# Eighteen rows of one head and batch to a partition, and key sums in four row tiles

## The chip, the cores and the metric

The kernel runs on one core of a Trainium2 chip. The metric is device time in microseconds of one execution, without the profiler; the number given for a kernel is the median of its runs. A profile is one execution of its own, taken with the hardware profiler on; its span runs from the first instruction to the last.

## What is computed

A linear attention ("hedgehog" features) feeds a spectral mixing layer. There are 8 batches, 8 heads, 576 rows of a sequence and head dimension 64; the second stage sees 8 x 576 rows of 512 channels.

```python
def phi(x):                                   # 64 -> 128 -> 256 features
    proj = np.einsum('bhsd,df->bhsf', x, w_phi)
    proj = proj - np.max(np.abs(proj), axis=-1, keepdims=True)
    return np.concatenate([np.exp(proj), np.exp(-proj)], axis=-1)
q_p, k_p = (phi(q), phi(k))
kv = np.einsum('bhsf,bhsd->bhfd', k_p, v)     # the key sums
z = np.sum(k_p, axis=2)
num = np.einsum('bhsf,bhfd->bhsd', q_p, kv)
den = np.einsum('bhsf,bhf->bhs', q_p, z)[..., None] + 1e-06
x = (num / den)                               # then (batch, row, 512)
...
X = np.fft.rfft(x, axis=1)                    # 64 lowest modes, w_r and w_i per mode
Yr = Xr @ w_r - Xi @ w_i;  Yi = Xr @ w_i + Xi @ w_r
u = x + np.fft.irfft(Y, n=S, axis=1)
out = u + np.maximum(u @ w_ch, 0.0)
```

The weights `w_r` and `w_i` are 64 x 512 x 512 each in float32, 134 MB together; q, k and v are 9.4 MB each, and so is the output.

## The kernel before

**Units.** The attention is cut into 16 units: a unit is two heads (group `g` of 4) of two batches (pair `bp` of 4). A tile of q, k or v has 128 partitions of 18 rows of 64. Before, partition `64 h + p` holds rows `9 p` to `9 p + 8` of head `h`, first of one batch and then of the other, so a load has two runs of 9 rows (2304 B in memory) for each partition (`load`, lines 94 to 98). q and k are cast to bf16 on the way, v stays float32. The source's axes come in the order row group (128), batch (2), run (576); the tile's in the order partition (128), batch (2), run (576).

**The loop.** One loop (lines 534 to 612) runs over steps `n`, and in a step four units are at different stages. Unit `n + 2` ("R") is transposed on PE (`turn_k`, `turn_q`, copied out by ACT). Unit `n + 1` ("K") has its projections and their maxima (`rows_k`, `rows_q`: PE, then DVE) and the exponentials of the keys (`exp_k`, tiles `AB` and `ABr`, on ACT). Unit `n` ("Q") has v weighted by the maxima (`weigh_v2`, DVE, tile `va`), the queries' projections and exponentials (`cols_q`, `exp_q`, tiles `AQ` and `AQr`), the key sums (`kv`, copied out by `keep_kv` into `kvz`), and the numerators and denominators (`num`, in three parts). Unit `n - 1` ("P") goes through the forward transform (`freq`, `keep_x`). Each engine keeps the order in which the program issues its work (class `InOrder`).

**Loads and queues.** POOL issues k and q of unit `n + 4`, v of unit `n + 2` and the weights, each in the step as it stands in the loop; they share POOL's software DMA queue. v of units 0 and 1 (line 383 and 386) and of unit 15 (`load_v_parts`, line 113, in pieces of 57, 64 and 7 partitions) are issued on SP, whose queue also carries the stores. A weight tile `wt` is 1024 KB in bf16, read from 2 MB in float32; there are 64 of them, nine buffers, and some places that are free early (`home`). A tile is asked for again when a tile has been used (`some`, `next_w`).

**PSUM.** In the loop, tiles named `two` take two banks and there are two of them; tiles named `one` take one bank and there are four. A step uses `two` in this order: `rows_k(0)`, `cols_q(1)`, `rows_k(1)`, `rows_q(0)`, `rows_q(1)`, `cols_q(0)`; a use waits for the reader of the use two places before it. The key sums go to two `one` tiles, one for each head:

```python
for h in range(2):
    r = slice(64 * h, 64 * h + 64)
    pe.matmul(
        pk[h][:, i, ab, :], lhsT=self.AB[n // 8][r, ab, n % 8, :],
        rhs=self.va[r, ab, n, :],
        start=(i == ab == c == 0), stop=(i == ab == 1 and c == 8),
    )
```

so that two matmuls of 64 rows, on the two halves of PE's rows, follow each other; 72 of them for a unit.

**The second stage.** After the loop the rest of the weights is mixed in (`mix`), and between the mixes the channel products (`Channels`) and the inverse transform (`Absorb`) are done. What needs the last weights follows in `finish`, and the output rows are written in `Pair.store` on SP: pairs of row places are written as one DMA of 512 KB (in two halves for the first three pairs), and the ninth place of each partition (`n8`) in DMAs of its own. Which row of the sequence stands at which place also enters the tables of the transforms (`si`, `nine`, `tok`) and the places that `back`, `freq` and `store` name.

Of the kernel before, what the change touches and what calls it, by code (L numbers as in the profile page):

```python
# [43 lines left out]
def kernel(  # L44
# [49 lines left out]
    def load(t, src, g, bp, eng):  # L94
        eng.dma_start(
            t.rearrange("p b c d -> p b (c d)"),
            src[2 * bp:2 * bp + 2, 2 * g:2 * g + 2].rearrange("b h (p c) d -> (h p) b (c d)", c=9),
        )


    class Unit:
# [3 lines left out]
        def load_k(self):  # L105
            self.kb = pin.tile([128, 2, 9, D_], BF16, name="kb")
            load(self.kb, k, self.g, self.bp, pool)

        def load_q(self):
            self.qb = pin.tile([128, 2, 9, D_], BF16, name="qb")  # L110
            load(self.qb, q, self.g, self.bp, pool)

        def load_v_parts(self):
            self.vn = pin.tile([128, 2, 9, D_], F32, name="vn")
            dst = self.vn.rearrange("p b c d -> p b (c d)")
            src = v[2 * self.bp:2 * self.bp + 2, 2 * self.g:2 * self.g + 2].rearrange(
                "b h (p c) d -> (h p) b (c d)", c=9)
            for p0, p1 in ((0, 57), (57, 121), (121, 128)):
                sp.dma_start(dst[p0:p1], src[p0:p1])

        def load_v(self, eng=pool):
            self.vn = pin.tile([128, 2, 9, D_], F32, name="vn")
            load(self.vn, v, self.g, self.bp, eng)

        def turn(self, src, dst, flat, part):

            rows = src.rearrange("p i c d -> p (i c d)")
            lo, hi = ((0, 4), (4, 9))[part]
            ptr = one([128, hi - lo, 128], BF16)
            for j in range(lo, hi):  # L130
                if flat or j < 4:
                    pe.transpose(ptr[:, j - lo, :], rows[:, j * 128:(j + 1) * 128], ident_b)
                elif j < 8:
                    n = 9 + 2 * (j - 4)
                    pe.transpose(ptr[:, j - lo, :], rows[:, n * 64:n * 64 + 128], ident_b)
                else:
                    for i in range(2):
                        pe.transpose(ptr[64 * i:64 * i + 64, j - lo, :], src[:, i, 8, :], ident_b)
# [51 lines left out]
        def weigh_v2(self):  # L190
# [3 lines left out]
            for ab in range(2):  # L194
                dve.tensor_tensor(
                    out=self.va[:, ab, :, 0:64], in0=self.vn.rearrange("p i c d -> p (i c) d"),
# [4 lines left out]
        def kv(self):  # L201
            pk = [one([128, 2, 2, 65]) for h in range(2)]
            for i in range(2):
                for ab in range(2):
                    for c in range(9):
                        n = 9 * i + c
                        for h in range(2):
                            r = slice(64 * h, 64 * h + 64)
                            pe.matmul(
                                pk[h][:, i, ab, :], lhsT=self.AB[n // 8][r, ab, n % 8, :],  # L210
                                rhs=self.va[r, ab, n, :],
                                start=(i == ab == c == 0), stop=(i == ab == 1 and c == 8),
                            )
            self.pk2 = pk

        def keep_kv(self):
            for h in range(2):
                act.copy(self.kvz[:, h], self.pk2[h])
# [41 lines left out]
        def exp_q(self, i):  # L260
            if i == 0:
                self.AQ = []
            if i < 2:
                t = pm.tile([128, 2, 2, 2, 2, 64, 2], BF16, name="AQ", bufs=3)
            else:
                t = pm.tile([128, 2, 2, 128], BF16, name="AQr", bufs=1)
            for ab in range(2):
                if i < 2:
                    o = t[:, ab].rearrange("f c j h p a -> f a c (j h) p")
                    src = self.pa.rearrange("f c (a j) (h p) -> f a c (j h) p", a=2, h=2)  # L270
                else:
                    o, src = t[:, ab], self.pa
                act.activation(o, src, ACT.Exp, scale=1.0 - 2.0 * ab)
            self.AQ.append(t)

        def num(self, n0):

            pn = one([128, 6, 65])
            for n in range(n0, n0 + 6):
                h = n % 2  # L280
                if n < 16:
                    i, c = n // 8, n % 8 // 2
                    for ab in range(2):
                        pe.matmul(
                            pn[:, n - n0, :],
                            lhsT=self.AQ[i][:, ab, c % 2, c // 2, h].rearrange("f p a -> f (p a)"),
                            rhs=self.kvz[:, h, i, ab, :], start=(ab == 0), stop=(ab == 1),
                        )
                else:
                    for i in range(2):  # L290
                        r = slice(64 * i, 64 * i + 64)
                        for ab in range(2):
                            pe.matmul(
                                pn[r, n - n0, :],
                                lhsT=self.AQ[2][:, ab, i, 64 * h:64 * h + 64],
# [9 lines left out]
        def freq(self):  # L305
            g, bp = self.g, self.bp
            px = one([128, 4, 2, 2, 32])
            for i in range(2):
                for out, d, t in ((px[:, 0:4:3, :, i], 0, slice(0, 2)),
                                  (px[:, 2, :, i], 1, 0), (px[:, 1, :, i], -1, 1)):  # L310
                    for c in range(5):
                        n = 8 * i + 2 * c if c < 4 else 16
# [79 lines left out]
    for p0 in (0, 64):  # L392
        pool.iota(si[p0:p0 + 64, 4:5], [[1, 1]], base=8, channel_multiplier=9)
# [3 lines left out]
    pool.iota(nine.bitcast(I32), [[9, 64]], base=0, channel_multiplier=0)  # L397
# [22 lines left out]
    dve.tensor_scalar_mul(out=odd[:, 1:2], in0=odd[:, 0:1], scalar1=-0.5)  # L420
# [113 lines left out]
    for n in range(-2, len(units) + 1):  # L534
# [55 lines left out]
        elif R and n + 4 == len(units):  # L590
            kept = pin.tile([128, 2, 9, D_], BF16, name="kb").rearrange(
                "p b c d -> p (b c d)")[:, 0:1024].rearrange("p (f m) -> p f m", m=8)
# [84 lines left out]
    def inverse_tables():  # L677
# [11 lines left out]
        for i in range(2):  # L689
            dve.tensor_scalar_add(out=tok[:, 512 + 64 * i:576 + 64 * i], in0=nine, scalar1=8.0)  # L690
# [75 lines left out]

    def back(p, c, bp, table, src, r, start):

        if c < 8:
            pe.matmul(p, lhsT=table[r, c % 4, :], rhs=src[r, 2 * bp + c // 4, :],  # L770
# [98 lines left out]
    class Pair:  # L869
# [32 lines left out]
        def sums(self, side, a):  # L902
            (bp, n), at, z = self.items[a], self.at(side, a), self.z(side)
            start = not self.based(side)
            if self.straight:
                pe.matmul(at, lhsT=CM[n // 4][:, n % 4], rhs=ends[z], start=start,
# [29 lines left out]
        def store(self):  # L936
# [3 lines left out]
            for p in parts:  # L940
                a = slice(p[0], p[-1] + 1)
                self.add(a)
                if self.n8:
                    sp.dma_start(
                        bass.AP(tensor=out.tensor, offset=out.offset + (2 * bp * S_ + 8) * DMODEL,
# [206 lines left out]
```

## Time and profile before

| | |
|---|---|
| time, median of 3 runs | 431.36 us (430.62 to 431.5) |
| the profiled execution | 430.94 us, span 428.7 us |
| PE, DVE, ACT, POOL busy | 321.2, 303.6, 300.6, 127.8 us |
| bytes moved by DMA | 97.71 MB in 50040 packets, 228 GB/s on the mean |
| read from HBM, written | 163.64 MB, 9.44 MB |
| mean granted TensorE clock | 0.942 |
| key sums' matmuls (64 x 128, 65 columns) | 1152, mean 199 ns each, overlapping |
| ACT: `AQ`, `AB`, 128x1024 | 1347 ns (x64), 1051 ns (x64) |
| ACT: `kvz` copies, 128x260 | 438 ns (x32) |
| ACT: `AQr`, 128x256 | 384 ns (x32) |
| k, q, v loads on POOL's queue, issue to landing, median | 21.4, 19.7, 25.1 us |
| v on SP's queue, units 0 and 1, issue to landing | 4.6 us |

A busy time is the sum of an engine's instructions where they don't overlap; DMA issues, waits and register work are not in it. The 40 slices show each engine's busy share in tenths. The chain of waits is followed back from the last instruction: at each step to what released it. "Issue to landing" has the time in the queue in it, not only the transfer. A DMA leaves one record for each packet of data, and beside them small records of 4 B, with which it reports that its part on one DMA engine is done. bytes are counted where they are written: a weight's 4096 B of float32 become a packet of 2048 B.

### The profile page before, as it was taken

The page shows a single profiled execution, that of the slowest core. Times are in us where ns is not written, and L with a number is a line of the kernel's source. Part 1 is how long each engine was busy: PE and PEld are TensorE (multiplying, and loading weights), DVE is VectorE, ACT ScalarE, POOL GpSimd, SP SyncE. Part 2 cuts the span into 40 slices and gives each one's busy share as a digit, 9 for nine tenths or more (in the row PEclk, how much of TensorE's full clock was granted, in tenths as well). Part 3 has the DMA queues.
Part 4 walks back from the last instruction along what each step waited for, and adds up shares of the span by engine and source line. Part 5 has one row for each costly group of instructions (what it writes and reads, how often), then busy time and mean ns, then how long its engine had stood idle before and what let it go on. Part 6 is the DMA issues. An engine that isn't in the chain of part 4 may idle for free.

```text
span 428.7 us, 10215 instructions
## 1 busy us (share of the span) xinstructions
PE 321.2 (75%) x4243; PEld 195.5 (46%) x4291; DVE 303.6 (71%) x592; ACT 300.6 (70%) x490; POOL 127.8 (30%) x167
## 2 busy tenths in 40 slices
PE   1666676678696677786795767867899789878994
PEld 1345555456364445554564545543454333333321
DVE  6668668766776776877877858868645546964695
ACT  3788788896887996977978848766644335553883
POOL 6232132123121213213122321220122037691661
PEclk9989799989999998998989969898999989999998
DMA  9999999999999999999999999999999999999798
GB/s 215 209 211 211 237 214 238 219 231 238 240 210 230 220 238 238 238 210 240 210 240 218 232 240 233 212 211 213 212 212 212 212 212 212 212 212 194 190 398 344
DMA packets 50040, 97.71 MB, mean 228 GB/s; under 512 B 2379, under 2 KB 11723, under 8 KB 49995
## 3 DMA queue, kind: packets, MB, share of 16 engines
q0 software_dynamic: 45152, 85.27, 101.6%
q1 hardware_dynamic: 4682, 11.73, 7.6%
q8 instruction: 33, 0.54, 0.5%
q10 hardware_dynamic: 160, 0.07, 0.1%
q14 instruction: 13, 0.10, 0.1%
HBM read 163.64 MB, written 9.44 MB: 404 GB/s over the span
## 4 chain that ended last, share of the span: by engine, by line
DMA 34%; PE 24%; ACT 22%; DVE 14%; issue 4%; POOL 1%; ACTq 0%; POOLq 0%; DVEq 0%
DMA wt<-in_moe_w_i_dram 28%; ACT AQ L37 9%; PE one L37 8%; PE pt L37 8%; DMA kb<-in_k_dram 6%; ACT AB L37 6%; DVE m L37 6%; PE two L37 5%; PE pp L37 3%; ACT qT L37 2%; ACT XT L37 2%; DVE xw L37 2%; DVE mk L37 1%; DVE mT L37 1%; DVE xs L37 1%
## 5 line engine op out<-in xcount | busy, mean ns | idle before, releaser
L37 ACT ACTIVATE AQ<-two 128x1024 bf16<-128x1024 f32 x64 | 80.5, 1347 | 2.2 <-PE two L37 2.1
L37 ACT ACTIVATE AB<-two 128x1024 bf16<-128x1024 f32 x64 | 62.7, 1051 | 4.5 <-DVE mk L37 4.2
L37 DVE TENSOR_REDUCE m<-two 128x8 f32<-128x1024 f32 x32 | 39.1, 1223 | 19.9 <-PE two L37 19.6
L37 POOL DMA_DIRECT2D wt<-in_moe_w_i_dram x30 | 22.2, 739 | 85.3 <-PE one L37 44.1
L37 DVE TENSOR_REDUCE mk<-two 128x8 f32<-128x1024 f32 x32 | 38.9, 1219 | 9.4 <-PE two L37 9.4
L37 ACT CAST xw<-pt 128x512 bf16<-128x512 f32 x39 | 22.9, 586 | 31.8 <-PE pt L37 31.6
L37 DVE TENSOR_TENSOR va<-vn,ee 128x1152 bf16<-128x1152 f32 x32 | 42.8, 1383 | 1.8 <-DMA vn<-in_v_dram 1.8
L37 PE MATMUL pt<-wchb,xT 128*128 128x512 bf16 x135 | 37.8, 394 | 7.2 <-DVE xT L37 2.4
L37 PE MATMUL two<-w2blk,qT 128*128 128x256 bf16 x128 | 21.9, 299 | 24.0 <-ACT AQ L37 12.3
L37 POOL DMA_DIRECT2D wt<-in_moe_w_r_dram x32 | 23.6, 739 | 52.6 <-PE one L37 25.9
L37 PEld LDWEIGHTS <-xs 128*128 128x128 bf16 x624 | 31.2, 102 | 13.3 <-issue 6.8
L37 ACT COPY qT<-one 128x512 bf16<-128x512 bf16 (+1 forms) x32 | 19.0, 642 | 20.8 <-PE one L37 20.7
L37 PEld LDWEIGHTS <-qT 128*128 128x128 bf16 x144 | 14.5, 103 | 38.2 <-issue 34.9
L37 PEld LDWEIGHTS <-XT 128*32 128x32 bf16 x584 | 16.8, 148 | 29.8 <-issue 16.9
L37 POOL DMA_DIRECT2D kb<-in_k_dram x16 | 11.4, 713 | 62.1 <-PE one L37 47.8
L37 PE MATMUL two<-mT,minus 96*128 96x512 bf16 x64 | 26.2, 410 | 2.9 <-issue 0.7
L37 DVE TENSOR_TENSOR xs<-one,rd 128x384 bf16<-128x384 f32 x48 | 26.8, 557 | 1.6
L37 PE MATMUL one<-wt,XT 128*32 128x512 bf16 x272 | 23.9, 439 | 3.4 <-ACT XT L37 3.4
L37 DVE TENSOR_TENSOR xs<-pa,xs 128x512 bf16<-128x512 f32 x27 | 17.7, 685 | 12.1 <-PE pa L37 10.3
L37 PE MATMUL one<-kvz,AQ 128*128 128x65 bf16 x512 | 25.3, 200 | 1.1 <-ACT qT L37 0.8
L37 PEld LDWEIGHTS <-AQ 128*128 128x128 bf16 x512 | 22.6, 103 | 7.0 <-issue 3.0
L37 POOL TENSOR_TENSOR xw<-rl,xw 128x512 bf16<-128x512 f32 x20 | 22.7, 1169 | 7.9 <-ACT rl L37 7.6
(161 smaller groups left out, 733.5 us busy)
## 6 DMA issues: line engine op xcount, KB each, us to landing
wt<-in_moe_w_r_dram POOLq DMA_DIRECT2D x29, 1024.0 KB, 27.7
wt<-in_moe_w_i_dram POOLq DMA_DIRECT2D x27, 1024.0 KB, 28.0
out_dram<-of SPq DMA_DIRECT2D x15, 512.0 KB, 3.6
vn<-in_v_dram POOLq DMA_DIRECT2D x13, 576.0 KB, 25.1
kb<-in_k_dram POOLq DMA_DIRECT2D x16, 288.0 KB, 21.4
qb<-in_q_dram POOLq DMA_DIRECT2D x16, 288.0 KB, 19.7
xs<-in_moe_w_i_dram POOLq DMA_DIRECT2D x2, 1024.0 KB, 23.9
out_dram<-of SPq DMA_DIRECT2D x6, 256.0 KB, 4.1
```

The lines of the kernel that those rows point to most:

```text
L37: ins = f(*args, **kwargs)
```

## The change

A partition of q, k and v now holds 18 rows of one head and one batch: partition `64 b + 32 h + p` holds rows `18 p` to `18 p + 17` of head `h` and batch `b`. The run in memory is 4608 B. The source pattern of a load is now batch (2), row group (64), run (1152), and the tile's is partition (128), run (1152). v of unit 15 is loaded in four pieces (57, 7, 57 and 7 partitions) instead of three.

A head and batch is now 32 partitions, so the key sums contract 32 rows at a time, in four row tiles: 144 matmuls for a unit. Two of the four results stand in the two banks of one `two` tile and two in `one` tiles; `keep_kv` copies them in three instructions instead of two. A step's order of `two` tiles becomes `rows_k(0)`, `cols_q(1)`, `rows_k(1)`, the sums, `rows_q(0)`, `rows_q(1)`, `cols_q(0)`.

`turn` transposes nine blocks of 128 columns for q too (ten pieces before). `exp_q` writes `AQ` with a stride of four elements (two before) and `AQr` with a stride of two (none before). The places of rows in the tables and in the output change with the layout; the stores keep their sizes, but for the ninth place, where two batch pairs are now two DMAs of 256 KB instead of one of 512 KB. Setting up the tables takes a few more small instructions on DVE. The number of rows in PE's program goes from 8562 to 10834.

```diff
     def load(t, src, g, bp, eng):
         eng.dma_start(
-            t.rearrange("p b c d -> p b (c d)"),
-            src[2 * bp:2 * bp + 2, 2 * g:2 * g + 2].rearrange("b h (p c) d -> (h p) b (c d)", c=9),
+            t.rearrange("p c d -> p (c d)"),
+            src[2 * bp:2 * bp + 2, 2 * g:2 * g + 2].rearrange("b h (p c) d -> b (h p) (c d)", c=18),
         )
...
         def load_v_parts(self):
...
-                "b h (p c) d -> (h p) b (c d)", c=9)
-            for p0, p1 in ((0, 57), (57, 121), (121, 128)):
-                sp.dma_start(dst[p0:p1], src[p0:p1])
+                "b h (p c) d -> b (h p) (c d)", c=18)
+            for p0, p1 in ((0, 57), (57, 64), (64, 121), (121, 128)):
+                sp.dma_start(dst[p0:p1], src[p0 // 64, p0 % 64:(p1 - 1) % 64 + 1])
...
             for j in range(lo, hi):
-                if flat or j < 4:
-                    pe.transpose(ptr[:, j - lo, :], rows[:, j * 128:(j + 1) * 128], ident_b)
-                elif j < 8:
-                    n = 9 + 2 * (j - 4)
-                    pe.transpose(ptr[:, j - lo, :], rows[:, n * 64:n * 64 + 128], ident_b)
-                else:
-                    for i in range(2):
-                        pe.transpose(ptr[64 * i:64 * i + 64, j - lo, :], src[:, i, 8, :], ident_b)
+                m = j if flat or j > 7 else 2 * (j % 4) + j // 4
+                pe.transpose(ptr[:, j - lo, :], rows[:, m * 128:(m + 1) * 128], ident_b)
...
         def kv(self):
-            pk = [one([128, 2, 2, 65]) for h in range(2)]
-            for i in range(2):
+            low = two([128, 2, DMODEL])[:, :, 0:130].rearrange("p h (a d) -> p h a d", a=2)
+            high = [one([128, 2, 65]) for h in range(2)]
+            out = [low[:, 0], low[:, 1]] + high
+            for i in range(3):
                 for ab in range(2):
-                    for c in range(9):
-                        n = 9 * i + c
-                        for h in range(2):
-                            r = slice(64 * h, 64 * h + 64)
+                    for n in range(8 * i, min(8 * i + 8, 18)):
+                        for p in range(4):
+                            r = slice(32 * p, 32 * p + 32)
                             pe.matmul(
-                                pk[h][:, i, ab, :], lhsT=self.AB[n // 8][r, ab, n % 8, :],
+                                out[p][:, ab, :], lhsT=self.AB[i][r, ab, n % 8, :],
                                 rhs=self.va[r, ab, n, :],
-                                start=(i == ab == c == 0), stop=(i == ab == 1 and c == 8),
+                                start=(n == ab == 0), stop=(n == 17 and ab == 1),
                             )
-            self.pk2 = pk
+            self.pk2 = low, high
 
         def keep_kv(self):
+            low, high = self.pk2
+            act.copy(self.kvz[:, :, 0], low)
             for h in range(2):
-                act.copy(self.kvz[:, h], self.pk2[h])
+                act.copy(self.kvz[:, h, 1], high[h])
...
             if i < 2:
-                t = pm.tile([128, 2, 2, 2, 2, 64, 2], BF16, name="AQ", bufs=3)
+                t = pm.tile([128, 2, 2, 2, 2, 32, 4], BF16, name="AQ", bufs=3)
             else:
-                t = pm.tile([128, 2, 2, 128], BF16, name="AQr", bufs=1)
+                t = pm.tile([128, 2, 2, 2, 32, 2], BF16, name="AQr", bufs=1)
             for ab in range(2):
                 if i < 2:
-                    o = t[:, ab].rearrange("f c j h p a -> f a c (j h) p")
-                    src = self.pa.rearrange("f c (a j) (h p) -> f a c (j h) p", a=2, h=2)
+                    o = t[:, ab].rearrange("f c b h p a -> f c a (b h p)")
                 else:
-                    o, src = t[:, ab], self.pa
-                act.activation(o, src, ACT.Exp, scale=1.0 - 2.0 * ab)
+                    o = t[:, ab].rearrange("f b h p e -> f e (b h p)")
+                act.activation(o, self.pa, ACT.Exp, scale=1.0 - 2.0 * ab)
...
                 if self.n8:
+                    for i, (bp, n) in enumerate(self.items):
+                        sp.dma_start(
...
                     sp.dma_start(
-                        bass.AP(tensor=rows.tensor,
-                                offset=rows.offset + (n % 4 + p[0]) * DMODEL,
-                                ap=[[9 * DMODEL, 64], [4 * DMODEL, 2], [1, len(p) * DMODEL]]),
+                        bass.AP(tensor=rows.tensor, offset=rows.offset + (j + p[0]) * DMODEL,
+                                ap=[[18 * DMODEL, 32], [4 * DMODEL, 4], [1, len(p) * DMODEL]]),
                         self.o[:, a].rearrange("p a e -> p (a e)"))
```

## The prediction

> **What bounds the kernel now.** I read the page first: its slices, its queues and its chain.
>
> ```profile
> span 428.7 us, 10215 instructions
> ...
> PE   1666676678696677786795767867899789878994
> ...
> DMA  9999999999999999999999999999999999999798
> ...
> q0 software_dynamic: 45152, 85.27, 101.6%
> q1 hardware_dynamic: 4682, 11.73, 7.6%
> ```
>
> No compute engine is at 9 for long; the DMA engines are, in 37 slices of 40. q0 is the queue that POOL feeds: weights, k, q and most of v. To tell a saturated queue from a busy one I read the chain in order of time:
>
> ```profile
> 200.70 25.02 DMA wt<-in_moe_w_i_dram
> 226.25 26.74 DMA kb<-in_k_dram
> 253.52 30.95 DMA wt<-in_moe_w_i_dram
> ...
> 328.49 37.24 DMA wt<-in_moe_w_i_dram
> 366.01 27.12 DMA wt<-in_moe_w_i_dram
> ```
>
> A weight tile waits 25 to 37 us between issue and landing. In the trace's completion records a 1024 KB weight tile lands 4.95 us behind the one ahead of it, so five to seven tiles stand in the queue at any time. Until 200 us the chain runs through compute instead, but behind a full queue that only shortens the queue. The last weights land at 393.2 us and 34 us of output work follow. So the time is a DMA stream of 390 us plus that tail, if compute can keep up. Whether it can, the windows say:
>
> ```profile
> core 0: us, PE busy (x) PEld busy (x) DVE busy (x) ACT busy (x) POOL busy (x), PEclk, DMA share, GB/s
> ...
> 200.00:285.00 85.00, 63.99 (x1119) 44.09 (x1121) 64.00 (x116) 63.25 (x102) 19.15 (x25) 0.91 1.13 225
> 285.00:328.00 43.00, 36.54 (x292) 18.52 (x299) 29.27 (x100) 25.32 (x45) 6.97 (x9) 0.96 1.12 212
> 328.00:366.00 38.00, 32.82 (x231) 14.85 (x233) 21.17 (x43) 16.68 (x32) 13.60 (x15) 0.96 1.12 212
> 366.00:395.00 29.00, 23.05 (x210) 10.56 (x212) 20.05 (x35) 14.95 (x29) 18.59 (x20) 1.00 1.09 209
> ```
>
> From 285 to 395 us PE works 92.4 of 110 us: compute has at most 18 us of air there. In the attention loop one step takes 15.1 us by compute (AQ starts at 71.22 and 86.34 in the chain); from the first step at 24.2 us, 16.4 steps would end at 272 us, and the stream holds the loop until 285. That is another 13 us of air.
>
> **The loads: how many engines carry them.** This part decides. Before, the source pattern of a load starts with 128 rows; after, `b (h p) (c d)` starts with the 2 batches. What does a short leading count do? The trace has two rows for it, the hardware queue's packets in the first 6.5 us and from 247 to 260 us:
>
> ```profile
> q1 hardware_dynamic: 544, 1.18, 53.7%
> ```
>
> ```profile
> q1 hardware_dynamic: 282, 0.59, 13.5%
> ```
>
> The first is v of units 0 and 1: 512 data packets and 32 four-byte completions, 16 for each DMA. The second is v of unit 15 in pieces of 57, 64 and 7 rows: 256 data packets and 26 completions, which is 3 + 16 + 7. A piece runs on as many engines as the largest number up to 16 that divides its leading count. From 252.4 us on, the 57-row piece trickles at 5 to 6 packets per half microsecond, where all pieces together had made 36: three engines, each taking one such packet (106 ns) and one weight packet (154 ns) in turn. By this reading a load that leads with 2 runs on two engines. The Trainium skill's page "DMA: Bandwidth & Descriptors", in "Why a DMA increments its semaphore by 16 and not by 1", gives this rule (the largest count up to 16 that divides the slowest dimension of both patterns), puts hardware-queue DMAs on the lowest-numbered engines and moves software ones round by a cursor; the trace agrees on 3, 16 and 7, and no row shows a leading 2.
>
> Packet prices per engine: a weight packet (2048 B written) is 4.95/32 = 154.7 ns. A k load lands 1.43 us behind the DMA ahead, 16 packets of 1152 B, 89.4 ns each. A v load takes 1.41 us, 8 packets of 4608 B, 176 ns. A merged k packet of 2304 B is not in the trace: on the line through the first two it costs 173 ns, with two of the old ones as upper bound, 179. I take 173. If all sixteen engines carried it, the merge would save (179 - 173) x 8 x 32 loads = 1.4 us. On two engines a load is 64 packets, 11.1 us, on each of them.
>
> A weight tile needs all 16 engines, so the stream ends with its most loaded engine. I assume that v of units 0 and 1 fall on the same pair (if not: 11.3 us less on it), and that the 45 software loads go round the eight pairs, 5 or 6 each. Then for that pair:
>
> - v of units 0 and 1: 2 x 64 x 176 ns = 22.5 us, where 4.0 us (1.8 to 5.8 us) stood before: +18.5.
> - v of unit 15: 40 packets x 176 ns = 7.0 for 48 x 106 ns = 5.1: +1.9.
> - 32 k and q and 13 v loads: 32 x 1.43 + 13 x 1.41 = 64.1 us become 6 x 11.1 = 66.6, or 5 x 11.1 = 55.5: +2.5, or -8.6. I take 6, since the first load is likely to start at the first pair and 45 is five rounds and five pairs.
> - PE's program grows from 8562 to 10834 rows; at 0.54 MB for the former that is 9 more 16 KB fetches, 0.95 us each, over 16 engines: +0.5.
>
> The stream: +23.4 us, bounds +1 (different pairs and 5 loads) and +23.4.
>
> **Compute, behind that stream.** k of unit 0 shares its pair with v. Packets taken in turn, its 64 need 64 x (173 + 176) = 22.3 us: it lands near 27 us instead of 7.7, and the first transpose moves from 8.75 by about 18 us (with a pair of its own, 7). Then the key sums. They now also fill a "two" tile, of which there are two:
>
> ```profile
> 75.95 2.54 ACT L37 ACTIVATE AQ<-two 128x1024 bf16<-128x1024 f32 x2
> ...
> 75.98 0.97 PE L37 MATMUL one<-va,AB 64*128 64x65 bf16 x50
> ...
> 78.54 0.60 PE L37 MATMUL two<-w2blk,qT 128*128 128x256 bf16 x4 [1.23 <-ACT AQ L37]
> ```
>
> Before, the sums start beside AQ; after, their tile is the one that AQ reads, so they start at 78.5, in the 1.23 us that PE waits. That is free, but the next tile is late: the first q projection then needs the tile of AB, free at 80.3, not AQ's, 78.5: +1.8 us. DVE's maxima, shift, and the num matmuls queue behind it: about +1.9 us a step. The sums have 72 pairs of load and matmul now, two row tiles at a time, one pair of tiles each 32 ns (1.14 us); 144 in fours take the same 1.14 us if four run beside each other, 2.28 if only two do. No row shows four row tiles; the nearest, 128*32 weight matmuls in four column tiles, start 2 ns apart, so I take 1.14. ACT: three copies for two, with 128x130 between the rows of 36 (249 ns) and 260 elements (438): about 328, +0.22 us a unit; AQr to a stride, by AQ over AB (1347/1051): 384 to 492 ns, +0.22; AQ's stride doubles, between 1051 and 1643 ns, I keep 1347. One transpose less saves PE about 60 ns. Two more store issues on SP lie under 3.6 us of landing: 0 here, 0.5 each if SP were the bound.
>
> Loop end by compute: 272 + 18 + 16 x 1.9 = 320, 35 later than 285. The second stage can win back 7 us (the waits of PE and its loads for weights there) to 18: +17 to +28 at 395. The stream's +23.4 and this meet, so the later of the two is some 25 us. 430.9 (the profiled run, 0.4 under the median of 431.36) + 25 = **456 us**. Its own range is 440 to 474: below, five loads on the pair and a pair of its own for k; above, key sums that run only two tiles at a time (1.14 x 16 = 18 us) that the second stage takes in part.
>
> **Rivals.**
> - *All loads still use sixteen engines*, because the 128 partitions of the destination decide. For it: every software DMA here shows 16 completions (1888 for 118), though none leads with less than 16. The merge then saves 1.4 us, by packet durations (107 ns for 1152 B, 173 for 2048) as much as 5.7; the code fetch costs 0.5, and the loop's 30 us of waits fit into 13 + 18 us of air. **430.0 us**, 425 at best: not slower. It decides if a load of k still lands 1.4 us behind the DMA ahead of it. 0.11.
> - *Only the hardware queue narrows*, so that k and q stay short: +18.5 + 1.9 + 0.5 - 1.4: **450 us**. For it: the 3 and the 7 are both hardware rows. 0.09.
> - *The software loads don't go round* and all fall on one pair: 45 x 11.1 = 500 us for 64.1, **890 us**. Against it: nothing in the trace piles up. 0.04.
> - *Sixteen engines, but the loop's wait breaks through*: 30 us less only the loop's 13: **447 us**. 0.02.
>
> The forecast keeps 0.74. **Range 436 to 476**: it leaves out the first and third rival and 0.05 of the forecast. 0.2%, 0.9 us, is about what a measurement tells from no change: the first rival splits into 0.07 faster and 0.04 the same; slower 0.89.
>
> **What would show it.** Two completions for v of units 0 and 1 on the hardware queue, not 16; their packets until 25 to 50 us; the first transpose after 15 us; k loads that land up to 11 us behind their neighbours, with single engines busy while others idle (a DMA row below 9); the last weight near 415. The key sums starting at AQ's end shows the tile's wait, groups of four within some 10 ns the tiles. It is wrong if k lands in 1.4 us steps, and if the row of the DMA stays at 9 with the last weight at 392.

## The result, and the profile after

The changed kernel takes 580.31 us (median of 6 runs, 578.38 to 581.33) where the kernel before takes 431.35 (6 runs, 430.62 to 431.78): a ratio of 1.3453, interval 1.3426 to 1.348. The forecast was 456 us, in a range of 436 to 476. The direction was right, the size was not: 149 us more where 25 were forecast.

The profiled execution spans 578.8 us, 150.1 more than before's 428.7. First the slices and queues of its page, beside the rows that the prediction began with:

```profile
span 578.8 us, 12582 instructions
...
PE   0025464655766648476673756657567899799995
...
PEclk9997575756768596675776668676698899899998
DMA  8629999698679998877989899999989999696498
...
DMA packets 85886, 98.02 MB, mean 169 GB/s; under 512 B 42696, under 2 KB 43848, under 8 KB 85832
...
q0 software_dynamic: 81376, 85.43, 83.6%
```

The stream is no longer the bound. q0's packets took 101.6% of the span before and take 83.6% now, the DMA row has 6s, 7s and 8s, and a weight tile lands sooner after its issue, not later. Before, then after (the last number is the median from issue to landing, in us):

```profile
wt<-in_moe_w_i_dram POOLq DMA_DIRECT2D x27, 1024.0 KB, 28.0
...
wt<-in_moe_w_i_dram POOLq DMA_DIRECT2D x27, 1024.0 KB, 16.7
```

POOL shows it too: before, its instructions wait 37 us in all for weights to land, after not at all.

So the queue empties, and something else holds the loop. The window from 200 to 285 us (PE, PEld, DVE, ACT, POOL busy, then PE's granted clock, DMA share and GB/s) shows no engine full, and PE's clock at 0.72 where it had been 0.91:

```profile
200.00:285.00 85.00, 55.06 (x970) 36.86 (x970) 44.61 (x79) 65.86 (x82) 15.97 (x20) 0.72 0.90 157
```

That is a chain in which engines take turns. The chain of waits (start, duration, what) shows it over one step of the loop, from one unit's first `AQ` to the next one's. Before:

```profile
71.22 2.39 ACT AQ L37 x2
...
76.12 2.38 ACT AQ L37 x2
...
78.54 0.61 PE two L37 x4
...
79.17 1.23 DVE m L37
...
86.34 2.39 ACT AQ L37 x2
```

And after (the key sums are many small pieces; the first is kept here):

```profile
330.07 4.65 ACT AQ L37 x2
...
337.20 4.61 ACT AQ L37 x2
...
341.85 0.20 PE two L37 x2
...
342.94 1.95 ACT AB L37 x2
...
344.93 1.03 PE two L37 x4
...
345.97 1.22 DVE m L37
...
353.14 2.40 ACT AQ L37
```

The operation that has grown most, over the whole span, before and after (count, busy time, mean ns, idle time before):

```profile
L37 ACT ACTIVATE AQ<-two 128x1024 bf16<-128x1024 f32 x64 | 80.5, 1347 | 2.2 <-PE two L37 2.1
...
L37 ACT ACTIVATE AQ<-two 128x1024 bf16<-128x1024 f32 x64 | 152.3, 2529 | 2.2 <-PE two L37 2.2
```

Three stretches are to be compared. From the first pair of `AQ` to the end of the second: 76.12 + 2.38 - 71.22 = 7.28 us before, 337.20 + 4.61 - 330.07 = 11.74 after, 4.46 more. From there to DVE's maxima of `rows_q(0)`: 0.67 before, 4.16 after, 3.49 more: the key sums and `exp_k(1)` have come into the chain, and the projection itself takes 1.03 us where it took 0.61. From there to the next `AQ`: 7.17 both times. The step has grown by 7.95 us.

The rest is at the start. In the waits of the first 60 us, PE stands still for k and q of unit 0 (total, times, longest):

```profile
PE one L37 <- DMA kb<-in_k_dram: 32.7, 1, 32.7
...
PE one L37 <- DMA qb<-in_q_dram: 7.7, 1, 7.7
```

k of unit 0 lands at 32.6 us (8.1 before) and q at 41.4 (9.5 before). v of units 0 and 1 each report two completions now, at 26.0 and 26.5 and at 40.4 and 40.9 us, where 16 each stood before: the narrow loads that the prediction had named. In slices of 1 us, from 0 to 40 us, the DMA row falls to one tenth, some two of sixteen engines, from 28 to 35 us, while q of unit 0 and v of unit 1 were still on their way:

```profile
DMA  0036659999999999997555555553111111143222
```

The three stretches can be measured for all steps and all kernels from the starts and durations in the trace. The table gives the median time; the start of the first unit's first `AQ`; the three stretches as means over the 15 steps to the last unit's first `AQ` (a: to the end of the second pair of `AQ`; b: on to the start of DVE's maxima of `rows_q(0)`; c: on to the next unit's `AQ`); the mean step; and what follows from the last of these to the span's end.

| kernel | time, us | first AQ | a | b | c | step | behind |
|---|---|---|---|---|---|---|---|
| before | 431.35 | 24.1 | 7.46 | 0.99 | 8.13 | 16.58 | 155.9 |
| after | 580.31 | 55.5 | 11.82 | 4.61 | 8.09 | 24.52 | 155.5 |
| e1: after, loads on 16 engines | 549.98 | 26.2 | 11.81 | 4.46 | 8.15 | 24.42 | 156.4 |
| e2: after, AQ without stride | 504.71 | 54.5 | 6.56 | 4.91 | 8.06 | 19.53 | 156.1 |
| e3: e1 and e2 | 468.25 | 26.3 | 6.56 | 4.58 | 7.89 | 19.02 | 156.2 |
| e4: before, key sums in `two` | 474.10 | 24.1 | 7.42 | 4.20 | 8.05 | 19.66 | 152.6 |
| e5: before, AQ at a stride of four | 504.64 | 24.0 | 11.84 | 0.92 | 8.77 | 21.53 | 154.8 |
| e7: before, strided read | 432.09 | 24.1 | 6.69 | 1.24 | 8.84 | 16.77 | 155.5 |
| e8: e1 with strided read | 470.43 | 27.0 | 6.57 | 4.55 | 7.93 | 19.04 | 155.5 |
| e9: e4, one stock of tiles | 450.62 | 24.1 | 7.41 | 3.27 | 7.57 | 18.25 | 150.5 |
| e10: e8, one stock of tiles | 466.79 | 26.1 | 6.58 | 4.07 | 8.14 | 18.79 | 154.3 |
| e11: e8, sums in pairs, early | 507.49 | 26.0 | 9.42 | 3.33 | 8.76 | 21.51 | 158.1 |
| e12: e10, sums in pairs, later | 453.39 | 25.9 | 7.18 | 1.76 | 9.15 | 18.09 | 155.3 |
| e13: e7, one stock of tiles | 432.48 | 23.0 | 6.65 | 1.23 | 8.81 | 16.69 | 157.1 |
| e14: before, loads split | 436.65 | 25.3 | 7.79 | 0.91 | 8.46 | 17.17 | 151.2 |

For the changed kernel: 31.4 us more at the start, 15 x 4.36 = 65 in stretch a, 15 x 3.62 = 54 in stretch b, nothing in c and nothing behind the loop. That is the 150 us between the spans.

### The profile page after: what moved, and what is told of

Read it like the earlier page. It is cut to its first block, busy times and chain, and to the rows that moved or that the text cites. A ratio compares the mean times of both kernels' runs of the same rounds, so it can differ in the third digit from the quotient of the medians.

```text
span 578.8 us, 12582 instructions
## 1 busy us (share of the span) xinstructions
PE 370.5 (64%) x5427; PEld 220.7 (38%) x5427; DVE 302.0 (52%) x598; ACT 375.7 (65%) x506; POOL 133.2 (23%) x167
## 3 DMA queue, kind: packets, MB, share of 16 engines
q0 software_dynamic: 81376, 85.43, 83.6%
## 5 line engine op out<-in xcount | busy, mean ns | idle before, releaser
L37 ACT ACTIVATE AQ<-two 128x1024 bf16<-128x1024 f32 x64 | 152.3, 2529 | 2.2 <-PE two L37 2.2
L37 PE MATMUL two<-va,AB 32*128 32x65 bf16 x1024 | 30.3, 236 | 56.3 <-ACT AQ L37 56.3
L37 PE MATMUL two<-qT,w2blk 128*128 128x512 bf16 x64 | 31.1, 485 | 44.9 <-ACT AQ L37 44.9
L37 PEld LDWEIGHTS <-AB 32*128 32x128 bf16 x2048 | 29.3, 124 | 62.3 <-issue 62.3
L37 POOL DMA_DIRECT2D kb<-in_k_dram x16 | 13.4, 835 | 131.4 <-PE one L37 130.5
L37 PE MATMUL two<-w2blk,qT 128*128 128x256 bf16 x128 | 32.0, 399 | 16.5 <-ACT AB L37 15.3
L37 PE MATMUL one<-ident_b,kb 128*128 128x128 bf16 x144 | 19.2, 286 | 33.0 <-DMA kb<-in_k_dram 32.7
L37 ACT COPY kT<-one 128x512 bf16<-128x512 bf16 (+1 forms) x32 | 20.0, 635 | 30.8 <-PE one L37 30.7
L37 PEld LDWEIGHTS <-xs 128*128 128x128 bf16 x624 | 31.4, 103 | 12.4 <-issue 6.8
L37 ACT ACTIVATE AQr<-one 128x256 bf16<-128x256 f32 x32 | 12.3, 457 | 34.3 <-PE one L37 34.3
L37 DVE TENSOR_TENSOR XT<-one,side 128x256 bf16<-128x256 f32 x32 | 12.1, 420 | 39.9 <-ACT XT L37 37.8
L37 PEld LDWEIGHTS <-minus 96*128 96x128 bf16 x96 | 11.8, 123 | 53.2 <-issue 50.0
```

The source lines that it names most:

```text
L37: ins = f(*args, **kwargs)
```

## The experiments

Each group ran beside the kernel before on the same chip: 431.67 us for the first to fourth, 431.81 for the fifth to eighth, 432.33 for the ninth to eleventh, 432.19 for the twelfth and thirteenth, 431.41 for the last.

### e1: the loads on sixteen engines

```diff
-        eng.dma_start(t.rearrange("p c d -> p (c d)"),
-            src[2 * bp:2 * bp + 2, 2 * g:2 * g + 2].rearrange("b h (p c) d -> b (h p) (c d)", c=18))
+        for b in range(2):
+            eng.dma_start(t[64 * b:64 * b + 64].rearrange("p c d -> p (c d)"),
+                src[2 * bp + b, 2 * g:2 * g + 2].rearrange("h (p c) d -> (h p) (c d)", c=18))
```

> After, but each load of k, q and v is two DMAs of 64 partitions, one for each batch, so that no source pattern leads with 2. If the loads' two engines are the main cause (the forecast's step): about 440, and the DMA row at 9 again. If the stride of AQ is (2529 ns for 1347): only the late start goes, k of unit 0 lands near 9 us for 32.7 and the loop keeps its step of 23.5 us: 550 to 560.

549.98 us, ratio 1.2745 (1.2699 to 1.2792): 30 us of the 149. Nearly all of it is the start (first `AQ` at 26.2 us instead of 55.5); the step hardly moves (24.42 for 24.52), which is the second case. While the loop is slow, narrow loads hide in it.

### e2 and e3: AQ written without a gap

```diff
-                    o = t[:, ab].rearrange("f c b h p a -> f c a (b h p)")
+                    o = t[:, ab].rearrange("f c b h p a -> f (c b h p a)")
+                    src = self.pa.rearrange("f c n s -> f (c n s)")
```

and the same for `AQr`; e3 has e1's loads too, and its numerators stand in the same other order as those of e2.

> After, but AQ and AQr are written without a stride, in the order in which they are read (so the numerators use rows and columns in a wrong order). If the stride is the main cause: AQ at 1050 ns, 4 x 1.5 us less in a step, 16 steps: 580 - 95 = 485, or what the two-engine loads then allow, not under 455. If it is not: 570 or more, since ACT was busy 65% only.

> After with both edits: 16 engines for the loads and AQ without a stride. What is left is the key sums' wait for their two-bank tile, 144 matmuls and a third copy. If these are hidden, as forecast for a stream of 16 engines: 425 to 432. If the wait breaks through: 435 to 450.

e2 takes 504.71 us, 1.1675 (1.1604 to 1.1745): 76 us for the order in which the elements of `AQ` and `AQr` stand, 20 us short of its first case (485). `AQ` takes 1051 ns there, so this takes off 64 x 1.48 = 95 us of ACT's work, the 0.30 us of before's own stride among it. e3 takes 468.25, 1.0851 (1.0779 to 1.0922), outside both of its cases; the two parts add up (30 + 76 of the 112). Between e2 and e3 the loads' share is 36 us, 28.2 at the start and 15 x 0.51 in the loop: in a faster loop the narrow loads are no longer quite hidden. Some 37 us remain that neither part explains.

### e4: the key sums in a two-bank tile, alone

```diff
-            pk = [one([128, 2, 2, 65]) for h in range(2)]
+            both = two([128, 2, DMODEL])[:, :, 0:260].rearrange("p h (i a d) -> p h i a d", i=2, a=2)
+            pk = [both[:, h] for h in range(2)]
```

> Before, with the key sums (two row tiles of 64, as before) in the two banks of a two tile: the wait alone. The sums then start when AQ ends, not beside it, and a step is up to 1.9 us longer. If the air of 13 and 18 us takes it: 430 to 433. If not: up to 447.

474.10 us, 1.0987 (1.0962 to 1.1013), above both cases: 42 us for a tile's place in PSUM, in the kernel before with its 72 matmuls of 64 rows. The timeline (start, duration, what; in brackets what an engine had idled for) shows how:

```profile
129.99 2.52 ACT L37 ACTIVATE AQ<-two 128x1024 bf16<-128x1024 f32 x2
132.57 1.51 PE L37 MATMUL two<-va,AB 64*128 64x65 bf16 x50 [2.47 <-ACT AQ L37]
133.73 1.94 ACT L37 ACTIVATE AB<-two 128x1024 bf16<-128x1024 f32 x2 [1.21 <-PE two L37]
...
135.72 1.01 PE L37 MATMUL two<-w2blk,qT 128*128 128x256 bf16 x4 [1.03 <-ACT AB L37]
136.77 1.23 DVE L37 TENSOR_REDUCE m<-two 128x8 f32<-128x1024 f32 x1 [4.68 <-PE two L37]
```

PE waits 2.47 us for `AQ`'s tile. Then ACT, which had nothing to do with the sums, waits 1.21 us for PE: `AB` has three buffers and a unit takes two, so `exp_k(1)` of unit `n + 1` writes the buffer that holds the first `AB` tile of unit `n`, and these sums still read it. Only when its exponentials are done may `rows_q(0)` have its tile, and it runs at 1.01 us for 0.60: PE's granted clock is 0.50 from 132.7 to 139.5 us, from the end of PE's wait of 2.47 us on (0.83 over the span, 0.94 before; the first 50 sums take 1.51 us here, 0.97 before). That the wait brings the low clock is likely, since it comes so in nearly every step, but no run shows it by itself. The table has it all in stretch b: 4.20 us for 0.99.

### e5 and e6: the price of the stride

e5 writes `AQ` in the kernel before at a stride of four elements; e6 writes the four `AQ` operations of a unit at one, two, four and eight:

```diff
+                    n = 2 ** (2 * i + ab)
+                    o = t[ab].rearrange("f c j h p a -> f (c j h p a)").rearrange("f (s n) -> f n s", n=n)
```

> The kernel before, its AQ numerators written at a stride of four elements (8 B) instead of two, nothing else changed; the numerators then stand in another order than the later matmuls read them, so the output is not the reference's. My theory: the write alone sets the price, so AQ takes 2.5 us as in the changed kernel (1.35 before), and since PE's two-bank tiles come free only at the end of AQ and AB, the loop's step grows by the whole 4 x 1.18 = 4.7 us, from 15.1 to about 19.8. 16 steps are 75 us, less the 13 us of air that the loop has and up to 18 us behind it: 475 to 493 us. Rival: ACT has room (63.25 of 85 us busy from 200 to 285 us), so only what goes beyond the step counts: 0.74 x 15.1 + 4.7 = 15.9 us for 15.1, 13 us in all, which the air takes: 431 to 436 us. Second rival: the price belongs to the changed kernel's lower clock or its neighbours, and AQ stays below 1.64 us: 431 us.

> The kernel before, with its four AQ operations of a unit written to four tiles at strides of one, two, four and eight elements (2, 4, 8 and 16 B) by the same ACT instruction, 128x1024 each; the numerators then stand in another order, so the output is not the reference's. Only the four durations are read. Theory: the price follows how far apart the written elements lie, in steps of 4 B or more: 1.05, 1.35, 2.5 us as seen so far, and 4.9 us at 16 B if it goes on doubling. Rival: a write of its own for every element is the worst there is, so eight costs what four costs, 2.5 us.

e5 takes 504.64 us, 1.1676 (1.1619 to 1.1733): 73 us, above the 475 to 493 of the theory. Its step grows by 4.95 us, 4.38 of it in stretch a, and nothing of that is given back by the air that the theory allowed for. ACT's groups in e6, which ran once (operation, shapes and count, busy time and mean ns, idle time before):

```profile
L37 ACT ACTIVATE AQh<-two 128x1024 bf16<-128x1024 f32 x16 | 77.4, 4838 | 0.0
...
L37 ACT ACTIVATE AQd<-two 128x1024 bf16<-128x1024 f32 x16 | 40.0, 2499 | 0.1
...
L37 ACT ACTIVATE AQb<-two 128x1024 bf16<-128x1024 f32 x16 | 21.4, 1334 | 0.0
...
L37 ACT ACTIVATE AQa<-two 128x1024 bf16<-128x1024 f32 x16 | 16.6, 1037 | 2.6 <-PE two L37 2.6
```

Strides of 2, 4, 8 and 16 B cost 1.04, 1.33, 2.50 and 4.84 us. From 4 B on this is a line: 1.17 us more for 4 B more, then 2.34 for 8 more, 0.29 us for each byte of stride. Carried back to 2 B that line gives 0.75 us, which is under the 1.04 that ACT takes anyway; so the first step of the ladder shows little of it (0.30 us), and the next two all. The rival of e6, that four elements apart is the worst there is, falls.

The Trainium skill's page "SBUF — State Buffer", in "Door 1: The DMA port swizzle (why `[64,N]` ≈ `[32,N]`)", says that SBUF's lines of 16 bytes let one stride free up to eight bf16 elements. For ACT's writes the runs say otherwise: 29% more at two elements, 2.4 times at four, 4.7 times at eight.

### e7 and e8: write without a gap, read at a stride

```diff
-                    o = t[:, ab].rearrange("f c j h p a -> f a c (j h) p")
-                    src = self.pa.rearrange("f c (a j) (h p) -> f a c (j h) p", a=2, h=2)
+                    o = t[:, ab].rearrange("f c j h p a -> f c (j h p) a")
+                    src = self.pa.rearrange("f c (a j) s -> f c (j s) a", a=2)
```

> The kernel before, with AQ written without a gap and PSUM read at a stride instead, the same values in the same places. Theory: ACT reads PSUM at any stride for nothing, so AQ takes 1.05 us instead of 1.35 and the step of the loop falls by up to 1.2 us; but the DMA stream bounds this kernel, so the time stays within 428 to 432 us. Rival: the strided read costs what the strided write did, AQ stays at 1.35 us or more, and the time is the same or, with AQ at 2.5 us, above 470 us. Second rival: the loop's step has a share in the time after all, and the kernel is 5 us or more faster.

> The changed kernel with each load of k, q and v as two of 64 partitions, and with AQ and AQr written without a gap and PSUM read at a stride instead: the same values in the same places. Theory: this is the third experiment with a right order of the numerators, so its time is the same, 466 to 472 us, AQ at about 1.05 us; what is left over the kernel before, some 36 us, belongs to the key sums' two-bank tile. Rival: a strided read costs like a strided write, AQ stays near 2.5 us, and the time is that of the first experiment, 550 us.

The same values reach the same places, and ACT now steps through PSUM, in e7 by 1 KB from one element to the next:

```profile
L37 ACT ACTIVATE AQ<-two 128x1024 bf16<-128x1024 f32 x64 | 62.6, 1044 | 2.6 <-PE two L37 2.6
```

That costs nothing over the 1037 ns of the operation without any stride in e6. e8 takes 470.43 us, 1.0867 (1.0825 to 1.0909), as e3 did, with the numerators where they belong. e7 takes 432.09, ratio 0.9997 (0.9983 to 1.0011): 18 us of ACT's work are gone and the time is the same, as the stream's bound says; what is saved turns into waiting, and POOL now waits 51 us in all for weights to land (37 before).

### e9 and e10: without AB's link

```diff
-                t = pm.tile([128, 2, 8, 128], BF16, name="AB", bufs=3)
+                t = slot([128, 2, 8, 128], "AB", self)
...
             Q.kv()
+            free("AB", Q)
...
             Q.num(12)
+            free("AQ", Q)
```

`slot` takes the first free one of six tiles that `AB` and `AQ` share; `AQ` draws from it in the same way. `exp_k(1)` now gets the tile that the unit before had used for `AQ`.

> The kernel before with its key sums in a two-bank tile, as in the fourth experiment (474 us), and with the six tiles of AB and AQ, three each before, drawn from one stock of six, so that exp_k(1) takes a tile that the unit before has done with and no longer waits for the key sums of this unit. Theory: the tile's wait alone delays rows_q(0) by the 1.9 us that I had forecast, and the rest of the fourth experiment's 5.3 us a step comes of exp_k(1), which ACT holds back until the sums have freed AB. So the step falls from 20.4 us to 17.0 or little above; the loop ends at 272 + 16 x 1.9 = 302 us, 17 later than 285, of which what follows takes up to 18: 431 to 448 us. Rival: the ring of two-bank tiles alone makes the wait (seven tiles to a step in place of six), and the time stays at 468 to 474 us. Second rival: PE's lower clock, once it idles, keeps the step long: 450 to 465 us.

> The changed kernel with sixteen-engine loads and the strided PSUM read (the eighth experiment, 470 us) and the one stock of six tiles for AB and AQ. Theory: the 36 us that are left over the kernel before are the key sums' wait, most of it by way of AB; without that link 435 to 452 us. Rival: the link has no share here, since the late tile alone does it: 466 to 470 us.

e9 takes 450.62 us, 1.0442 (1.0384 to 1.05): 23.5 of e4's 42 us go with the common stock of tiles, 14 of them in stretch b, 7 in c and 2 behind the loop. The timeline shows ACT going on without a wait:

```profile
122.31 2.52 ACT L37 ACTIVATE AQ<-two 128x1024 bf16<-128x1024 f32 x2
124.60 2.03 ACT L37 ACTIVATE AB<-two 128x1024 bf16<-128x1024 f32 x2
124.89 0.98 PE L37 MATMUL two<-va,AB 64*128 64x65 bf16 x50 [2.47 <-ACT AQ L37]
...
126.68 1.01 PE L37 MATMUL two<-w2blk,qT 128*128 128x256 bf16 x4 [0.40 <-ACT AB L37]
```

`rows_q(0)` starts as `AB` ends, the delay that the prediction had in mind; the step is 1.67 us over before's. The time is 2.6 us above the theory's 448 and in the range of the second rival, PE's low clock (450 to 465); stretch b keeps 3.27 us, AB's 2.03 and the projection at the low clock among them. e10 gains only 3.6 us over e8 (466.79; 1.0792, 1.076 to 1.0823): the rival's case. Its chain tells why:

```profile
165.60 1.14 DVE mk L37
166.83 1.95 ACT AB L37 x2
168.82 1.03 PE two L37 x4
```

With `AQ` at 1.05 us, ACT is ready for `exp_k(1)` before DVE has the keys' maxima (`mk`), which stand behind DVE's share of `keep_x`. From the end of `AQ` to the start of `AB` it waits 0.44 us on average, where in e8 it had waited 1.05, mostly for the sums: a new wait took nearly half of the old one's place.

### e11 and e12: the key sums without a two-bank tile

One batch at a time, so that two one-bank tiles are enough, and `keep_kv` behind each. In e11 the first half stands ahead of the second `cols_q` and the second behind it, in e12 (with e9's stock of tiles) ahead of `rows_k(1)` and behind `rows_q(0)`:

```diff
+        def kv(self, b):
+            pk = [one([128, 2, 65]) for h in range(2)]
...
+                        for h in range(2):
+                            r = slice(64 * b + 32 * h, 64 * b + 32 * h + 32)
...
+            Q.kv(0)
         some(1 if X and not end else 0)
             K.rows_k(1)
             K.exp_k(1)
+            K.rows_q(0)
+            Q.kv(1)
```

> The changed kernel with sixteen-engine loads and the strided PSUM read, and with the key sums taken one batch at a time into two one-bank tiles each, before and behind the second cols_q, so that they never use a two-bank tile. Two row tiles of 32 now run side by side in place of four, some 1.14 us more PE time a unit. Theory: the wait for the two-bank tile is the whole rest, so the time is that of the DMA stream again: 428 to 440 us. Rival: the 144 matmuls and three copies, or the later start, carry the 36 us: 455 to 470 us.

> The tenth experiment (467 us) with the key sums of one batch at a time in two one-bank tiles: batch 0 in front of rows_k(1), where va has long been there (the eleventh had put it in front of the second cols_q, where PE waited for va), batch 1 behind rows_q(0). No key sum uses a two-bank tile, and rows_q(0) again waits for AQ's tile instead of AB's. Theory: that wait of 1.9 us a step, with PE's low clock behind it, is the rest of the 35 us; the mean step falls from 18.8 to at most 17.2 us and the time to 430 to 443 us. Rival: 144 matmuls for 72, three or four copies for two and the 45 added load issues on POOL carry the rest; then the step stays at 18 us or more and the time at 455 to 470 us.

e11 is a miss: 507.49 us, 1.1706 (1.164 to 1.1773), slower than what it was to mend. Its chain has 7% in "DVE va" and 26% in "PE one": the sums stood where `va` had only just been asked for, and held up the projection behind them on PE. It says nothing of the tile. e12, with the sums later, takes 453.39 (1.0487, 1.0447 to 1.0527), 13.4 us under e10 and between its two cases. So the tile's wait is a part of what e10 left, and 21 us over the kernel before remain. Stretch b falls from 4.07 to 1.76 us, more than the 1.9 of the theory, but c gives back 1.01, with the second half of the sums and its copies in it now, and the mean step of 18.09 us is the rival's (18 or more). That mean has one odd step in it. It takes 28.5 us, the others 17.35 on average, and all that a has gained lies there: a is 16.1 us in this step and 6.55 in the others, as in e10. The waits from 250 to 290 us say why:

```profile
DVE XT L37 <- POOL kb L37: 9.1, 1, 9.1
ACT XT L37 <- POOL kb L37: 8.9, 1, 8.9
...
POOL wt L37 <- DMA wt<-in_moe_w_i_dram: 4.7, 1, 4.7
POOL qb L37 <- DMA wt<-in_moe_w_i_dram: 4.3, 1, 4.3
...
POOL vn L37 <- DMA wt<-in_moe_w_r_dram: 3.5, 1, 3.5
```

`keep_x` of this step may write `XT` only when POOL has copied the part of it that is still needed into a buffer of `kb`. The copy stands in POOL's order behind load issues, and these wait for weights to land. So the stream is back, by way of POOL: the step is 8.6 us longer than the same one before (19.9 us).

### e13 and e14: is the kernel before bound by its stream?

e13 is the kernel before with e7's read and e9's stock of tiles; e14 only splits its loads by batch, as e1 does, though each half keeps 128 partitions:

```diff
-            src[2 * bp:2 * bp + 2, 2 * g:2 * g + 2].rearrange("b h (p c) d -> (h p) b (c d)", c=9),
+        for b in range(2):
+            eng.dma_start(t[:, b].rearrange("p c d -> p (c d)"),
+                src[2 * bp + b, 2 * g:2 * g + 2].rearrange("h (p c) d -> (h p) (c d)", c=9))
```

> The kernel before with the strided PSUM read (1.2 us less ACT work a step) and the one stock of six tiles for AB and AQ: two compute links of the loop eased at once. Theory: the DMA stream is the bound of the kernel before, so the time stays within 429 to 433 us, with the last weight of the stream where it was. Rival: the loop's compute has a share in the end, and the time falls below 427 us.

> The kernel before with each load of k, q and v through POOL as two, one for each batch, still on sixteen engines: 45 more issues and nothing else. It is a control for the repair of the loads that experiments eight, ten, eleven and twelve share. Theory: the issues lie in POOL's idle time and the bytes and packets are the same, so 430 to 434 us, and the 21 us that the twelfth experiment left belong to the changed layout itself. Rival: the added issues hold back the weights behind them on POOL, 440 to 452 us, and the rest belongs to the repair.

e13 takes 432.48 us, ratio 1.0008 (0.999 to 1.0027): two links of the loop eased, no gain. The last weight lands at 397.5 us (395.8 before), and POOL waits 63 us in all for weights to land (37 before, 51 in e7; none in e4 and e5). So the stream is what bounds the kernel before. e14 takes 436.65, 1.0128 (1.0101 to 1.0155), between its cases: 45 issues more on POOL, and two on SP, cost 5 us with the same bytes. POOL waits 93 us in all for weights to land, as in e12 (96), and the wait of e12's odd step is there too, where before had 0.3 us (ACT, from 238 to 262 us):

```profile
ACT XT L37 <- POOL kb L37: 4.6, 1, 4.6
```

So some 5 of e12's 21 us may belong to the repair of the loads, and perhaps more: e14's halves still have 128 partitions, those of e12 have 64, and v's packets of 4608 B take 268 ns (median) in e12 for 178 in e14 and before. The rest is open. The doubled matmuls and the added copies were not tried by themselves. None of these kernels beats the kernel before.

## Why the prediction was wrong, point by point

- **"AQ's stride doubles, between 1051 and 1643 ns, I keep 1347."** This is the step that failed most. `AQ` takes 2529 ns. The upper bound came from carrying on the 296 ns that the first doubling had cost; but those 296 ns are what shows of a cost that grows with the stride above a floor that ACT has anyway (e6). 64 x 1.18 = 76 us, and e5, which adds just this to the kernel before, costs 73: nearly the whole price is in the time. (That e2 gives 76 too is chance: it takes 95 us off ACT.) It lies on the path because two pairs of `AQ` operations stand in the chain of every step and the two-bank tiles are freed only at its end; the prediction had itself shown PE waiting for that end.
- **"That is free, but the next tile is late ... about +1.9 us a step."** The lateness itself was right: with AB's link gone (e9) the step grows by 1.67. What was missed is that ACT is held up too: `exp_k(1)` stands behind the sums by way of `AB`'s three buffers, and the tile that is "next" is freed only after it. The step's chain grew by 3.49 us there, and the wait alone cost the kernel before 42 us (e4). The price of PE's clock was not in the sum either: 1.03 us for 0.61 in `rows_q(0)`.
- **The air.** 13 us in the loop and 7 to 18 behind it were set against the delays. Behind the loop nothing came back: 155.9 us before, 155.5 after, and at best some 5 less in an experiment (e9, e14). In the loop, air would show as a stretch c that shrinks when a step gets longer; it is 8.13 us before and 8.09 after, and 7.57 at the least (e9), 8 us over the loop. The 15.1 us "by compute" came from a step ahead of the fifth, where `some` mixes nothing yet (`X` is 0 for `n < 4`); later steps carry three mixes. That the stream binds the kernel before is right in the other direction: where ACT is eased, c grows to 8.8 us (e7, e13) and takes back what a had saved. (By the trace the last weight lands at 395.8 us, not 393.2, with 33 us behind it; no term hangs on this.)
- **"The stream: +23.4 us."** That the loads narrow was right. A load that leads with 2 shows in q0's count: 36,224 packets more than before's 45,152 are 45 loads x 14 engines x 64 four-byte records (40,320, by count), less the 4,096 that merging saved; and v of units 0 and 1 report two completions each. The Trainium skill's page "DMA: Bandwidth & Descriptors", in "Why a DMA increments its semaphore by 16 and not by 1", has the rule; this trace agrees with it for 2. But the stream stopped being the bound as soon as the loop was slower than it, so the sum for the most loaded pair never came to decide. What the narrow loads cost, 30 us (e1), is the start: 31.4 us for the 18 of the prediction, since not only k but also q of unit 0 is late (32.7 and 7.7 us of waiting). The prediction let the software loads go round the pairs; with two of sixteen engines busy from 28 to 35 us, q of unit 0 rather stood on v's pair or waited behind it. The trace doesn't name the engines, so which it was stays open. That no single pair takes all of them follows from the time: 500 us of loads and the weights beside them would not fit into 579 (an estimate, by the prediction's packet prices).
- **Right:** the direction; that k of unit 0 is late (that v's packets are what delays it fits the times, but no engine is named); nine more code fetches (33 packets before, 42 after); the four row tiles. In the last unit, at full clock, a group of four sums takes 32.5 ns, as a pair took before; 144 matmuls in 1.93 us in the loop are the lower clock, not two tiles behind two. The third copy and `AQr` (457 ns where 492 were forecast) are small, as costed.
- **The rivals.** Sixteen engines (430 us), the hardware queue alone (450), one pair for all (890) and sixteen with the wait broken through (447) all turned on the loads. Only the last let the loop's wait through, at 17 us over the stream, and e3 and e8, which are its case without the stride, stand 37 to 39 over it. None had the write of `AQ`. Shares of busy time could not have shown it: ACT is at 63.25 of 85 us before and at 65.86 after. The chain of one step does.

So of the 149 us about 75 are the strided write, 30 to 36 the two-engine loads, and about 37 are left for the key sums. This division is not quite like for like: e2 and e3 write `AQ` in 1.05 us where the kernel before takes 1.35, so a part of their gain was never the change's cost, and the share of the key sums may be larger by as much. e4 shows that the tile by itself can make it: alone it costs 42. In the changed kernel e10 and e12 take back 17 us. Of the 21 that e12 leaves, some 9 are the odd step's wait for POOL, which the repair of the loads brings (e14); the others were not separated from the slower packets of v and from what e12's own way of summing costs.

## What to carry to other kernels

When a tile's owner changes, follow one step of the chain by hand through every buffer that the delayed instruction holds, its inputs' as well as its output's, and add up the chain, not the engines' shares. A cost that has been seen at one size over a floor can't be carried on from that size; a ladder of three sizes costs one run. And where a layout needs a stride on one side of an ACT instruction, put it on the read from PSUM: here it costs nothing, where on the write it cost 75 us.

## What was not expected of the hardware

- From 4 B on, ACT's bf16 write grows by 0.29 us for each byte of stride in an operation of 1024 elements a partition (1.33, 2.50, 4.84 us at 4, 8, 16 B; 1.04 at 2 B), while the same values read from PSUM 1 KB apart take 1.04 us, as without any stride.
- Software-queue loads that lead with 2 add four-byte records, by count 64 for each of fourteen engines and each of 45 loads: records under 512 B rise from 2379 to 42696.
- v's packets of 4608 B take 178 ns (median) in loads of 128 partitions and 268 in halves of 64 partitions (e14, e12).
- Four row tiles of 32 x 128 run beside each other with 65 columns: 32.5 ns for a group of four at full clock, 53.6 ns where the clock had fallen.
- Where PE waits more, it is also granted less clock: 0.78 over the span for 0.94, and four projections of 256 columns in 1.03 us for 0.61.
